# A two-layer linear-attention block on one core: the second layer's first weights are placed and split during the attention product, and operand places move

## The chip, the cores and the metric

The kernel runs on one core of a Trainium2 chip. A core has five engines with queues of their own: PE (matmul), DVE (vector), ACT (scalar), POOL and SP; all transfers run on 16 shared DMA engines, and here SP's queue issues the loads and POOL's queue most stores. The metric is the device time of one execution in microseconds, the median of several runs. Before the change it is 2347.4 us (three runs, 2346.8 to 2353.08).

## The reference

`x` is [1, 2048, 1024], all in fp32. D = 1024, F = 3584, 32 heads of 32.

```python
x = A_x
xn = _layernorm(x, axis=-1)
s = _A_ref(xn, A_wqkv, A_wo)                 # linear attention, then @ wo
g = _silu(_B_ref(xn, B_w1, B_w3, B_w2))      # (silu(xn@w1) * (xn@w3)) @ w2
return x + s * g
...
pq, pk = phi(q), phi(k)
kv = jnp.einsum("bhsd,bhse->bhde", pk, v)
z = jnp.einsum("bhsd->bhd", pk)
num = jnp.einsum("bhqd,bhde->bhqe", pq, kv)
den = jnp.einsum("bhqd,bhd->bhq", pq, z)[..., None] + 1e-6
o = num / den
return (lambda x, *d: x.transpose(*d))(o, 0, 2, 1, 3).reshape(B, S, D) @ wo
```

## The kernel before

*Arithmetic.* Every large product is cut in 2 by 2 blocks and done with seven block products in place of eight (their names are in PRODUCTS: B11, T2, T3, T1, B21, T4, B22 for the right operands, and their partners A11, S2, S3, S1, A12, A22, S4 for the left ones). Each fp32 operand is split in two fp32r parts: `split` (L91) makes the high part with a cast on ACT (L95) and the low part with a subtract on DVE (L96). `mm3` (L100) then does three matmuls: left high by right high (L103), left high by right low (L104), left low by right high (L105). So the first two of a product need only the cast of the left operand, and the third needs its subtract.

*Stages.* First q, k, v and gate and up products over two halves of the tokens, with intermediate results in DRAM. Then two right-hand products, both done by the class `Segment` (L1001): the attention product `attention` ("s", nk = 4: queries divided by their denominators times the weights merged with wo), and the second layer, cut in five segments `layers` ("B0" with nk = 2, "B1" to "B4" with nk = 3), which add up in the sums `acc`. B0 follows directly on the attention product.

*A segment.* `right(k)` (L1010) loads, places and splits the seven right operands of step k. `operands(m)` (L1017) loads and splits the seven left operands of token group m (256 tokens; there are NG = 8 groups): these are called XA11, XS2 and so on, with raw loads rA11, rS2. `tokens(m, ...)` (L1033) does the group's products in PSUM banks a, b, c, d and adds them up with ACT and DVE in u and the four sums. Group 0 of a segment is done "outer": over k first and over the seven products within, so that only the operands of one k must be there at a time. `run` (L1220) goes over the groups, one group ahead with `operands(m + 1)`; at the last group it calls `ahead()`, and in every group `around(m)` if given. So while PE does group m, the other engines prepare group m + 1.

*Names in the profile.* Buffer numbers are left out: `XA11s` is a left operand of the attention product, `XA11B` one of a second-layer segment; `as`, `bs`, `cs`, `ds` are its PSUM banks, `us` and `s` its sums, and `aB` to `dB`, `uB`, `acc` those of the second layer. `B<-rB11B` and `T<-rT2B` are splits of second-layer weights; `wp` are the attention product's right operands, split in the same way.

*Places.* Tiles come from pools. `pb` (8 places of 4 KB per partition) holds left operands, `pe` (3) u, `pc` ("c" 6 places: `small`; "sg" 4 places: `signed`) sums and raw loads. `pa` holds the operands of the first stages and then `wp`; `praw` raw loads; `st` little things. `pa`, `praw` and `st` are opened in `era1` and closed after the attention product (L1266). Only then is `pw` opened, at their addresses, for the second layer's right operands (`layer_place`, L1269) and `acc`. So `layers[0].right(0)` (L1278) stands behind the whole attention product; `ask_first` (L1160) has four of its seven raw loads issued during the last attention group, two into spare `pe` places and two into `small` ones. The constant tile "gap" (L63) does no work; it moves all later addresses.

*What sets the order.* A scheduler orders the instructions of each engine when the program is built, and engines are then in order: an instruction that waits holds up all behind it on its engine, and a load that waits for its place to be free holds up all later loads of SP's queue.

Of the kernel before, what the change touches and what calls it, by code (L numbers as in the profile page):

```python
# [9 lines left out]
F32 = mybir.dt.float32  # L10
FR = mybir.dt.float32r
# [5 lines left out]
P = 128  # L17
C = 512
# [4 lines left out]
def tile_linear_attention_times_swiglu(  # L23
# [23 lines left out]
    const = ctx.enter_context(tc.tile_pool(name="const", bufs=1))  # L47
# [12 lines left out]
    for i in range(P // DH):  # L60
        nc.vector.memset(hmask[i * DH:(i + 1) * DH, i * DH:(i + 1) * DH], 1.0)

    const.tile([P, 79], F32, name="gap")  # L63
    zacc = const.tile([P, ND], F32, name="zacc")
    nc.vector.memset(zacc, 0.0)

# [2 lines left out]
    PRODUCTS = ["B11", "T2", "T3", "T1", "B21", "T4", "B22"]  # L69
# [21 lines left out]
    def split(pair, src, bias=None):  # L91

        hi, lo = pair[:, 0], pair[:, 1]
        if bias is None:
            nc.scalar.copy(out=hi, in_=src)  # L95
            return nc.vector.tensor_sub(out=lo, in0=src, in1=hi.bitcast(F32))  # L96
        nc.scalar.activation(hi, src, AF.Identity, bias=bias)
        return nc.vector.scalar_tensor_tensor(lo, src, bias, hi.bitcast(F32), op0=ALU.add, op1=ALU.subtract)
# [9 lines left out]
    pb = ctx.enter_context(tc.tile_pool(name="pb", bufs=8))  # L108
    pe = ctx.enter_context(tc.tile_pool(name="pe", bufs=3))
    pc = ctx.enter_context(tc.tile_pool(name="pc", bufs=6))  # L110
    era1 = ExitStack()
    pa = era1.enter_context(tc.tile_pool(name="pa", bufs=1))
    praw = era1.enter_context(tc.tile_pool(name="praw", bufs=2))
    st = era1.enter_context(tc.tile_pool(name="st", bufs=2))

    def small(name):
        return pc.tile([P, C], F32, tag="c", name=name)
# [189 lines left out]
    def columns(w, c0, n):  # L307
        return w[:, c0:c0 + n].rearrange("(k p) n -> p k n", p=P)
# [3 lines left out]
    class Operands:  # L312
# [10 lines left out]
        def ask(self):  # L323
            if self.raw is None:
                self.raw = praw.tile([P, ND, 2 * P], F32, tag="raw", name=f"w{self.name}")
                fetched[:] = [nc.sync.dma_start(out=self.raw, in_=columns(self.w, self.c0, 2 * P))]
# [86 lines left out]
    jobs = []  # L413
# [561 lines left out]
    for h in range(NH):  # L975
        order = [(part, pair) for part in (1, 0) for pair in range(ND // 2)]
        if h:
            order = [(part, pair) for pair in range(ND // 2) for part in (1, 0)]
        some = [Operands(wqkv, part * D + pair * 2 * P, f"{'qk'[part]}{h}_{pair}_", h == 0 and part == 1,
                         h and part == 0 and pair == 0)  # L980
                for part, pair in order]
# [17 lines left out]
    NG = S // GT  # L999
    PARTNER = {"B11": "A11", "T2": "S2", "B21": "A12", "T3": "S3", "T1": "S1", "T4": "A22", "B22": "S4"}  # L1000
    class Segment:  # L1001


        def __init__(self, name, nk, first, last, place, right, left, acc, end=None):
            self.last, self.U = last, {}
            self.name, self.nk, self.first = name, nk, first
            self.place, self.right_of, self.left_of, self.acc, self.end = place, right, left, acc, end
            self.Y, self.X = {}, {}

        def right(self, k):  # L1010

            for i, n in enumerate(PRODUCTS):
                raw = self.right_of(n, i, k)
                self.Y[n, k] = self.place(n, i, k)
                split(self.Y[n, k], raw)
# [130 lines left out]
    def hiddens(i, m):  # L1146
        return left(m, lambda n: h_d[i][m // NT][:, PLACE[n][m % NT]], (FB[i][1] - FB[i][0]) // 2, f"B{i}")
# [7 lines left out]
    def second_weights(i, n, k):  # L1155
        if (i, n, k) not in asked:
            ask(i, n, k, small)
        return asked[i, n, k]

    def ask_first():  # L1160

        for n, place in zip(PRODUCTS, (spare, spare, small, small)):
            ask(0, n, 0, place)

    def spare(name):
        return pe.tile([P, C], F32, tag="u", name=name)
# [53 lines left out]
    def run(seg, nxt=None, ahead=None, around=None):  # L1220

        def between(k):
            if m == NG - 1 and nxt:
                if k == 0:
                    nxt.operands(0)
                    for e in range(seg.nk, nxt.nk):
                        nxt.right(e)
                if k < nxt.nk:
                    nxt.right(k)

        if not seg.X:
            seg.operands(0)
        for m in range(NG):
            if m + 1 < NG:
                seg.operands(m + 1)
            elif ahead:
                ahead()
            if around:
                around(m)
            seg.tokens(m, m == 0 or m == NG - 1 and nxt is not None, between)  # L1240
# [13 lines left out]
    def attention_place(n, i, k):  # L1254
# [3 lines left out]
    attention = Segment("s", ND // 2, True, True, attention_place,  # L1258
                        attention_right, queries, lambda m, t, n: small(f"s{m}_{t}{n}"), store_s)
    attention.operands(0)  # L1260
    for k in range(attention.nk):
        attention.right(k)
    run(attention, ahead=ask_first)
    assert all(next(j, None) is None for j, _ in jobs)
    jobs.clear()
    era1.close()  # L1266
    pw = ctx.enter_context(tc.tile_pool(name="pw", bufs=1, reuse_waits="tile"))

    def layer_place(n, i, k):  # L1269
        return pw.tile([P, 2, C], FR, tag=f"{n}_{k}", name=f"{n}_{k}")  # L1270

    acc = []
    layers = [Segment(f"B{i}", (f1 - f0) // 2, i == 0, i == len(FB) - 1, layer_place,
                      lambda n, _, k, i=i: second_weights(i, n, k),
                      lambda m, i=i: hiddens(i, m), lambda m, t, n: acc[m][:, t, n],
                      finish if i == len(FB) - 1 else None)
              for i, (f0, f1) in enumerate(FB)]
    layers[0].right(0)  # L1278
    layers[0].operands(0)
    for k in range(1, layers[0].nk):  # L1280
        layers[0].right(k)
    acc.extend(pw.tile([P, 2, 2, C], F32, tag=f"acc{m}", name=f"acc{m}") for m in range(NG))
    for i, seg in enumerate(layers):
        run(seg, layers[i + 1] if i + 1 < len(layers) else None, around=lay_x if i == 2 else None)

# [22 lines left out]
```

## Time and profile before

| what | value |
|---|---|
| median of three runs | 2347.4 us |
| the profiled execution | 2349.84 us |
| its span (first to last instruction) | 2348.1 us |
| mean granted TensorE clock | 0.996 |
| DMA traffic | 479.69 MB, mean 204 GB/s |

The profile is of one execution, which was somewhat slower than the median; a sum of parts is made against its span and then carried over to the median. Times in timeline rows are microseconds from the start of the span: start, duration, engine, line, operation, output<-inputs, shapes, and in brackets how long the engine had stood idle before and what ended that. Ends of matmuls are modelled (0.39 us each), so the pitch from start to start says how fast PE goes. SPq rows are loads being issued, not their landing. Some matmul records are missing from the trace, a few per cent, so counts of matmuls are taken from the program.

### The profile page before, as it was taken

The page shows a single profiled execution, that of the slowest core. Times are in us where ns is not written, and L with a number is a line of the kernel's source. Part 1 is how long each engine was busy: PE and PEld are TensorE (multiplying, and loading weights), DVE is VectorE, ACT ScalarE, POOL GpSimd, SP SyncE. Part 2 cuts the span into 40 slices and gives each one's busy share as a digit, 9 for nine tenths or more (in the row PEclk, how much of TensorE's full clock was granted, in tenths as well). Part 3 has the DMA queues.
Part 4 walks back from the last instruction along what each step waited for, and adds up shares of the span by engine and source line. Part 5 has one row for each costly group of instructions (what it writes and reads, how often), then busy time and mean ns, then how long its engine had stood idle before and what let it go on. Part 6 is the DMA issues. An engine that isn't in the chain of part 4 may idle for free.

```text
span 2348.1 us, 30976 instructions
## 1 busy us (share of the span) xinstructions
PE 2300.6 (98%) x10368; PEld 1890.5 (81%) x10368; DVE 1780.3 (76%) x2830; ACT 924.7 (39%) x1639; POOL 689.8 (29%) x854
## 2 busy tenths in 40 slices
PE   6999999999999999999999999999999999999997
PEld 5788888888887888777888888888887888888876
DVE  8887888888777775657867788887745666766798
ACT  5555343433232555433332433334324534242433
POOL 4220333376866221001423344342310000000033
PEclk9999999999999999999999999999999999999999
DMA  6555455576668646776756666665656566665688
GB/s 233 179 184 180 153 184 184 170 226 218 226 209 314 221 146 202 253 258 203 224 180 183 191 193 212 205 213 174 224 158 196 180 188 176 222 215 177 192 267 258
DMA packets 353695, 479.69 MB, mean 204 GB/s; under 512 B 24208, under 2 KB 262800, under 8 KB 353424
## 3 DMA queue, kind: packets, MB, share of 16 engines
q1 hardware_dynamic: 315808, 357.63, 48.2%
q0 software_dynamic: 37728, 120.09, 15.6%
q8 instruction: 81, 1.33, 0.2%
q14 instruction: 78, 0.64, 0.1%
HBM read 306.71 MB, written 174.59 MB: 205 GB/s over the span
## 4 chain that ended last, share of the span: by engine, by line
PE 73%; issue 5%; DVE 4%; DMA 3%; ACT 1%; POOL 0%; SPq 0%; DVEq 0%; POOLq 0%; ACTq 0%
PE g L103 2%; PE g L104 2%; PE g L105 2%; PE dB L104 1%; PE dB L105 1%; PE dB L103 1%; PE aB L103 1%; PE cB L103 1%; PE cB L104 1%; PE aB L104 1%; PE aB L105 1%; PE cB L105 1%; PE bB L105 1%; PE bB L104 1%; PE bB L103 1%
## 5 line engine op out<-in xcount | busy, mean ns | idle before, releaser
L750 POOL DMA_DIRECT2D h_d<-sg x112 | 82.8, 740 | 256.8 <-DVE sg L746 166.3
L1063 POOL DMA_DIRECT2D u_d<-uB x32 | 17.3, 541 | 407.6 <-DVE uB L1046 345.8
L96 DVE TENSOR_TENSOR xy<-xy,xy 128x512 fp32r<-128x512 f32 x112 | 72.9, 686 | 65.4 <-ACT xy L95 65.3
L95 ACT CAST xy<-xy 128x512 fp32r<-128x512 f32 x112 | 65.1, 619 | 102.0 <-PE g L105 58.4
L104 PE MATMUL g<-xy,xy 128*128 128x512 f32 x224 | 87.8, 392 | 0.3 <-DVE xy L96 0.2
L105 PE MATMUL g<-xy,xy 128*128 128x512 f32 x224 | 87.3, 390 | 0.0
L103 PE MATMUL g<-xy,xy 128*128 128x512 f32 x224 | 82.7, 398 | 0.0
L517 POOL DMA_DIRECT2D y_d<-y x48 | 34.6, 721 | 140.0 <-ACT y L537 79.9
L1046 DVE TENSOR_TENSOR acc<-cB,acc 128x512 f32<-128x512 f32 x50 | 34.4, 689 | 42.9 <-PE cB L105 42.9
L1046 DVE TENSOR_TENSOR acc<-dB,acc 128x512 f32<-128x512 f32 x56 | 38.6, 689 | 30.8 <-PE dB L105 30.6
L730 POOL TENSOR_TENSOR hs<-hs,sg 128x256 f32<-128x256 f32 x56 | 60.5, 1081 | 0.1
L732 POOL TENSOR_TENSOR hs<-sg 128x256 f32<-128x256 f32 x56 | 57.3, 1023 | 0.0
L103 PEld LDWEIGHTS g<-xy,xy 128*128 128x128 f32 x224 | 41.8, 188 | 14.2 <-issue 4.5
L888 POOL DMA_DIRECT2D qs_d<-qd x32 | 18.1, 564 | 117.5 <-DVE qd L884 80.1
L1177 POOL DMA_DIRECT2D s_d<-s x32 | 17.3, 541 | 117.4 <-DVE s L1046 69.2
L733 POOL TENSOR_TENSOR hs<-sg,hs 128x256 f32<-128x256 f32 x56 | 50.6, 903 | 1.4
L104 PEld LDWEIGHTS g<-xy,xy 128*128 128x128 f32 x224 | 42.1, 188 | 10.2 <-DVE xy L96 1.4
L729 POOL TENSOR_TENSOR hs<-sg,sg 128x256 f32<-128x256 f32 x56 | 49.7, 887 | 1.2
L765 POOL TENSOR_TENSOR w<-w 128x256 f32<-128x256 f32 x28 | 28.2, 1007 | 73.0 <-DMA w<-in_B_w 73.0
L105 PEld LDWEIGHTS g<-xy,xy 128*128 128x128 f32 x224 | 42.1, 188 | 8.8
L758 POOL DMA_DIRECT2D h_d<-hs x60 | 45.8, 765 | 3.5 <-POOL hs L733 2.4
L95 ACT CAST XS4B<-rS4B 128x384 fp32r<-128x384 f32 (+1 forms) x40 | 19.7, 493 | 60.7 <-PE cB L105 41.1
(5315 smaller groups left out, 8326.9 us busy)
## 6 DMA issues: line engine op xcount, KB each, us to landing
h_d<-hs POOLq DMA_DIRECT2D x60, 256.0 KB, 3.3
h_d<-sg POOLq DMA_DIRECT2D x56, 256.0 KB, 3.7
w<-in_B_w SPq DMA_DIRECT2D x56, 256.0 KB
wt_d<-w SPq DMA_DIRECT2D x28, 512.0 KB
xy<-x_d SPq DMA_DIRECT2D x28, 512.0 KB
xy<-y_d SPq DMA_DIRECT2D x28, 512.0 KB
h_d<-hs SPq DMA_DIRECT2D x52, 256.0 KB
y_d<-y POOLq DMA_DIRECT2D x48, 256.0 KB, 3.1
```

The costliest lines, as they stand in the source:

```text
L95: nc.scalar.copy(out=hi, in_=src)
L96: return nc.vector.tensor_sub(out=lo, in0=src, in1=hi.bitcast(F32))
L103: nc.tensor.matmul(acc, lhsT=wh, rhs=ah, start=start, stop=False, skip_group_check=True)
L104: nc.tensor.matmul(acc, lhsT=wh, rhs=al, start=False, stop=False, skip_group_check=True)
L105: return nc.tensor.matmul(acc, lhsT=wl, rhs=ah, start=False, stop=stop, skip_group_check=True)
L729: e.tensor_add(out=s1, in0=a21, in1=a22)
L730: e.tensor_sub(out=s2, in0=s1, in1=a11)
L732: e.tensor_sub(out=s3, in0=a11, in1=a21)
L733: e.tensor_sub(out=s4, in0=a12, in1=s2)
L750: nc.gpsimd.dma_start(out=h_d[i][2 * h + c][:, 2 * n:4 * n + 2, k], in_=src)
L758: queue.dma_start(out=h_d[i][2 * h + c][:, 6 + 4 * e:10 + 4 * e, k], in_=o[e].rearrange("p (e s) -> p e s", s=P))
L1046: return V.tensor_add(out=c, in0=src, in1=c)
```

## The change

`pa` moves from era1 into an era of its own and to the right end of SBUF; `praw` and `st`, now alone on the left, are closed before the attention product runs, once its last raw weights are split. Their room becomes `pw0`, which holds the seven k = 0 right operands of the second layer and acc0. During attention groups 2 to 6 a new hook, `first_weights`, calls `layers[0].right(0)` for one or two of the seven products (products 0 and 1 in group 2, 2 in group 3, 3 and 4 in group 4, 5 in group 5, 6 in group 6). At the last group `ask_next` issues four early loads as `ask_first` did, but for k = 1. The rest of the right operands and sums stay in `pw`, which takes the place of `pa`, on the right, after the attention product. An "edge" tile of 8 floats and a "gap" of 47 instead of 79 floats set the addresses: operand places, all at 64 modulo 512 before, are all at 448 modulo 512 after.

```diff
-    const.tile([P, 79], F32, name="gap")
+    const.tile([P, 47], F32, name="gap")
...
-    era1 = ExitStack()
-    pa = era1.enter_context(tc.tile_pool(name="pa", bufs=1))
+    era1, era2 = ExitStack(), ExitStack()
+    ctx.enter_context(tc.tile_pool(name="edge", bufs=1, side="right")).tile([P, 8], F32, name="edge")
+    pa = era2.enter_context(tc.tile_pool(name="pa", bufs=1, side="right"))
...
-        def right(self, k):
-
-            for i, n in enumerate(PRODUCTS):
+        def right(self, k, some=range(7)):
+
+            for i in some:
+                n = PRODUCTS[i]
                 raw = self.right_of(n, i, k)
...
-    def ask_first():
+    def ask_next():
 
         for n, place in zip(PRODUCTS, (spare, spare, small, small)):
-            ask(0, n, 0, place)
+            ask(0, n, 1, place)
...
-    run(attention, ahead=ask_first)
-    assert all(next(j, None) is None for j, _ in jobs)
+    era1.close()
     jobs.clear()
-    era1.close()
-    pw = ctx.enter_context(tc.tile_pool(name="pw", bufs=1, reuse_waits="tile"))
+    pw0 = ctx.enter_context(tc.tile_pool(name="pw0", bufs=1, reuse_waits="tile"))
+    pw = []
 
     def layer_place(n, i, k):
-        return pw.tile([P, 2, C], FR, tag=f"{n}_{k}", name=f"{n}_{k}")
+        return (pw[0] if k else pw0).tile([P, 2, C], FR, tag=f"{n}_{k}", name=f"{n}_{k}")
...
-    layers[0].right(0)
+
+    def first_weights(m):
+        if 2 <= m < NG - 1:
+            layers[0].right(0, [i for i in range(7) if i * 5 // 7 == m - 2])
+
+    run(attention, ahead=ask_next, around=first_weights)
     layers[0].operands(0)
+    era2.close()
+    pw.append(ctx.enter_context(tc.tile_pool(name="pw", bufs=1, side="right", reuse_waits="tile")))
     for k in range(1, layers[0].nk):
         layers[0].right(k)
-    acc.extend(pw.tile([P, 2, 2, C], F32, tag=f"acc{m}", name=f"acc{m}") for m in range(NG))
+    acc.append(pw0.tile([P, 2, 2, C], F32, tag="acc0", name="acc0"))
+    acc.extend(pw[0].tile([P, 2, 2, C], F32, tag=f"acc{m}", name=f"acc{m}") for m in range(1, NG))
```

## The prediction

> **What bounds the kernel now.** The page first: TensorE is busy for almost the whole span, so only time in which it stands still can be won.
>
> ```profile
> span 2348.1 us, 30976 instructions
> PE 2300.6 (98%) x10368; PEld 1890.5 (81%) x10368; DVE 1780.3 (76%) x2830; ACT 924.7 (39%) x1639; POOL 689.8 (29%) x854
> ```
>
> Then the busy time by stage (columns: stretch, length, then busy us and count of PE, PEld, DVE, ACT, POOL; granted clock, DMA share, GB/s). The stretches are the attention product, the change to the second layer, the rest of its first segment, its middle segments, its last one.
>
> ```profile
> 1640.90:1793.26 152.36, 151.79 (x669) 125.13 (x667) 82.41 (x122) 45.86 (x80) 28.86 (x45) 1.00 0.57 178
> 1793.26:1830.00 36.74, 32.70 (x137) 24.72 (x136) 27.82 (x52) 21.88 (x48) 2.16 (x4) 1.00 0.81 263
> 1830.00:1869.40 39.40, 39.40 (x176) 32.66 (x175) 21.94 (x46) 22.18 (x51) 2.16 (x4) 1.00 0.54 160
> 1869.40:2250.00 380.60, 380.60 (x1681) 315.57 (x1680) 273.22 (x471) 141.44 (x270) 21.77 (x32) 1.00 0.63 195
> 2250.00:2341.00 91.00, 83.94 (x365) 67.82 (x363) 83.16 (x140) 34.42 (x65) 28.99 (x33) 1.00 0.97 295
> ```
>
> PE is full in the attention product and from 1830 to 2250, and has holes from 1793 to 1830 and in the last segment, where the DMA engines are 97% busy. The change works in the first of these. The timeline of PE there, begun with two matmuls of the steady stream before it:
>
> ```profile
> 1779.66 0.39 PE L103 MATMUL cs<-wp,XS3s 128*128 128x512 f32 x1
> 1793.03 0.39 PE L105 MATMUL ds<-wp,XS4s 128*128 128x512 f32 x1
> 1793.26 0.39 PE L103 MATMUL B11B<-B,XA11B 128*128 128x512 f32 x1
> 1794.80 0.50 PE L104 MATMUL B11B<-B,XA11B 128*128 128x512 f32 x1 [0.93 <-DVE B L96]
> 1798.87 0.50 PE L103 MATMUL B22B<-B,XS4B 128*128 128x512 f32 x1 [1.03 <-ACT B L95]
> 1802.28 0.50 PE L103 MATMUL T2B<-T,XS2B 128*128 128x512 f32 x1 [0.38 <-ACT T L95]
> 1819.68 0.50 PE L103 MATMUL cB<-T,XS3B 128*128 128x512 f32 x1 [1.64 <-ACT XS3B L95]
> 1826.42 0.50 PE L103 MATMUL aB<-B,XA11B 128*128 128x512 f32 x1
> ```
>
> The first two rows are 59 starts apart: 13.37 / 59 = 0.2266 us each. In PE's order of the built program 120 matmuls lie between the starts at 1793.26 and 1826.42; they should take 27.19 us and take 33.16, so 5.97 us are lost. The waits at 1794.80, 1798.87 and 1802.28 are for weights of the second layer (B, T); each costs its idle time, 0.16 (the modelled end, 0.39, hides that much beyond the pitch) and 0.11 (the start behind it takes 0.50 in place of 0.39): 0.93 + 1.03 + 0.38 + 3 x 0.27 = 3.15 in all. The rest, some 2.8, hangs on the left operands of the next token groups (XS3B, XA11B).
>
> **The change, part by part.** *Moved:* seven weight loads of 256 KB, seven casts and seven subtracts (the k = 0 weights of segment B0). They now stand in attention groups 2 to 6, one or two a group. The k = 1 weights take their old places, and the four early loads fetch k = 1. The built program has the same instructions on every engine; the orders differ from attention group 2 to the fourth group of B0, and not elsewhere.
>
> Cost in the attention product:
>
> ```profile
> 1757.12 0.43 SPq L1153 DMA_DIRECT2D rB11B<-in_B_w  x1
> 1758.10 0.62 ACT L95 CAST XS2s<-rS2q 128x512 fp32r<-128x512 f32 x1 [2.10 <-PE as L105]
> 1758.75 0.69 DVE L96 TENSOR_TENSOR XS2s<-rS2q,XS2s 128x512 fp32r<-128x512 f32 x1 [2.03 <-ACT XS2s L95]
> 1758.62 0.58 ACT L1094 COPY us<-as 128x512 f32<-128x512 f32 x1
> 1775.40 0.54 POOL L1177 DMA_DIRECT2D s_d<-s  x1 [2.18 <-DVE s L1053]
> ```
>
> A split is 0.62 us of ACT and 0.69 of DVE, in gaps of some 2 us which recur with every product (2.72 us). On ACT the copy of `as` stands behind a weight's cast, which can wait for its load. Nothing needs that bank before B21 is added to it, three products or 8.2 us later; the slowest load below takes 5.5 us and is issued about 0.5 us before the group begins. On SP's queue only loads for the next group, 19 us away, stand behind. The `small` places that the weights take wait for stores of the group before, whose last is issued at 1775.40, 1.2 us into a group (group 7 begins at 1774.22, 84 matmuls before 1793.26), and lands some 3 us later, while a weight load comes at the group's end. So I price this at 0; what hides it is PE's own stream. Without that cover seven subtracts would cost 4.8 us.
>
> At the transition, the weights and what their loads depend on:
>
> ```profile
> 1794.07 0.68 DVE L96 TENSOR_TENSOR B<-rB11B,B 128x512 fp32r<-128x512 f32 x1
> 1794.66 0.69 DVE L96 TENSOR_TENSOR T<-rT2B,T 128x512 fp32r<-128x512 f32 x1
> 1798.20 0.62 ACT L95 CAST B<-rB22B 128x512 fp32r<-128x512 f32 x1 [1.02 <-DMA rB22B<-in_B_w]
> 1798.85 0.69 DVE L96 TENSOR_TENSOR B<-rB22B,B 128x512 fp32r<-128x512 f32 x1 [0.76 <-ACT B L95]
> 1797.93 0.32 SPq L1153 DMA_DIRECT2D rT3B<-wt_d  x1
> 1802.63 0.62 ACT L95 CAST T<-rT3B 128x512 fp32r<-128x512 f32 x1 [0.41 <-DMA rT3B<-wt_d]
> 1803.29 0.69 DVE L96 TENSOR_TENSOR T<-rT3B,T 128x512 fp32r<-128x512 f32 x1 [0.34 <-ACT T L95]
> ```
>
> The first four rows become k = 1 at the same times, since their loads wait for the same stores. PE has 21 matmuls of k = 0 ready and reaches k = 1 at 1793.26 + 21 x 0.2266 = 1798.02, its B22 at 1801.87, when the cast (to 1798.82) and the subtract (to 1799.54) are done. All 3.15 us of weight waits go. The last three rows become weights of segment B1, which PE does not need yet.
>
> *What is late next:* left operands of group 2. Their loads stand on SP behind waits for the splits of group 1.
>
> ```profile
> 1808.30 0.42 DVE L96 TENSOR_TENSOR XA12B<-rA12B,XA12B 128x256 fp32r<-128x256 f32 x1
> 1808.74 0.32 SPq L1135 DMA_DIRECT2D rS2B<-h_d  x1
> 1813.21 0.43 ACT L95 CAST XS2B<-rS2B 128x256 fp32r<-128x256 f32 x1
> 1813.96 0.39 SPq L1135 DMA_DIRECT2D rS3B<-h_d  x1
> 1819.22 0.40 ACT L95 CAST XS3B<-rS3B 128x256 fp32r<-128x256 f32 x1 [2.05 <-DMA rS3B<-h_d]
> 1820.11 0.32 SPq L1135 DMA_DIRECT2D rS4B<-h_d  x1
> 1825.61 0.41 ACT L95 CAST XS4B<-rS4B 128x256 fp32r<-128x256 f32 x1 [1.80 <-DMA rS4B<-h_d]
> ```
>
> These loads take 4.5, 5.3 and 5.5 us from issue to cast. In the new DVE order XS1B, three sums of acc0 and B1's T1 stand between the subtract of 1803.29 and XA12B. With 0.6 us from one long start to the next (1794.07 to 1794.66) and 0.4 for a short one, XA12B ends near 1807.2 instead of 1808.7. So rS2B goes out 1.5 us earlier and its cast is done near 1812.1. PE wants it as matmul 76: 1793.26 + 76 x 0.2266 = 1810.48. A new wait of 1.6 to 1.9, taken 1.75. XS3B: XA22B's subtract, five long operations later, ends near 1810.6 and lets rS3B go, so its cast ends near 1816.3; PE, delayed by 1.75, wants it (matmul 96) at 1816.8: 0. XA11B of group 3 (matmul 114, wanted near 1820.8): its load waits for XS1B's subtract, near 1817.5 (XS1B is loaded right behind XS3B), then takes 3 to 4.5 us: 0 to 1.5, taken 0.9. Slower starts behind waits (0.11 each) and small steps, 0.5. Sum lost 3.15 against 5.97: **2.8 us gained**. Bounds: 6.0 (no new wait, if loads take 3.5 us) and 0 (they take over 5.3 us throughout).
>
> *Addresses.* In the built program all operand places start at 64 modulo 512 before and at 448 after, so they lie to each other as they did. What a shift does to an engine is shown by one tile which already lies at 0 modulo 512, uk__342, beside one at 64:
>
> ```profile
> L447 ACT COPY uk__342<-ak__343 x1: 585/585/585, 23.1 to 23.1; 128x512 f32<-128x512 f32 x1
> L447 ACT COPY uk__365<-ak__366 x1: 587/587/587, 25.6 to 25.6; 128x512 f32<-128x512 f32 x1
> h_d<-sg POOLq DMA_DIRECT2D x56, 256.0 KB, 3.7
> s_d<-s POOLq DMA_DIRECT2D x12, 256.0 KB, 3.0
> q0 software_dynamic: 3296, 7.87, 29.6%
> ```
>
> 585 against 587 ns: nothing. No full-size matmul streams an operand from another address, and no transfer uses one; I take 0 for both, as for ACT. From above for transfers: a store of 256 KB in pieces of 512 bytes (h_d) lands after 3.7 us, one in whole rows of 2048 bytes (s_d) after 3.0, so being cut in four costs a row 23%, and a shift should not cost it more. From below a gain of as much is as open, but I have no reason for it.
>
> [...]
>
> **The rivals.** (A) *All of it comes back*: the loads get faster because seven fewer of them crowd the stretch from 1793 to 1830 (DMA share 0.81): 2347.4 - 6.0 = 2341.4. Against it: B1's loads move up into the room. (B) *The wait only moves*: the loads of groups 2 and 3 take 5.3 us or more, as rS3B and rS4B do, and what PE wins ahead it loses there: 2347.0. (C) *Slower, by the addresses*: transfers with a row at 448 take longer and the last segment, DMA 97% busy for 91 us (88 us of DMA work), is stretched. At 3.2% the gain is gone, from 11% the kernel is slower by 0.3%. At the bound of 23%: stores alone (29.6% of 108 us) 0.23 x 32 = 7.4, so 2352.0; all transfers 20.2, so 2364.8. For it: that stage leaves no room. Against it: the ACT row. A matmul slowed by the shift belongs here too: 0.1% of 2300 us is 2.3 us.
>
> **How the numbers follow.** The profiled execution took 2349.84 us for its span of 2348.1; less 2.8 that is 2347.0. Against the median of the runs, 2347.4, it is **2344.6**. Forecast 0.60 (its own range 2343.0 to 2346.4), A 0.11, B 0.15, C 0.14. 0.3% is 7.0 us, about what a measurement of this kernel can tell from no change (its runs lie 6.3 apart). Faster than that lies beyond even A: 0.04, for scatter. Slower than 2354.4: the upper part of C and scatter, 0.11. The same: 0.85. The range goes from just under A to the stores of C: 2341.0 to 2352.0.
>
> **What would show it.** Right: PE starts at a pitch of 0.2266 from 1793.26 to about 1810, first wait on XS2B of 1 to 2 us, no wait on B or T; full PE in the attention product with seven more splits in its gaps. Wrong: a wait of `cs` or `as` there (moved step not hidden), a matmul pitch other than 0.2266 or a longer landing of s_d<-s than 3.0 us (addresses), or a last segment that lasts longer than 91 us by more than its scatter.

## The result and the profile after

| kernel | median us | lowest to highest | runs |
|---|---|---|---|
| before | 2348.74 | 2346.64 to 2354.18 | 11 |
| after | 2343.29 | 2339.08 to 2346.91 | 11 |

The ratio is 0.9976, 95% interval 0.9966 to 0.9985: 5.5 us or 0.24% less, between 3.5 and 8.0 us by the interval. The forecast was 2344.6, a gain of 2.8 on the 2347.4 known then; the sign is right, the gain is about twice as large, and 2.8 lies just below the interval.

The page of the changed kernel, and its busy time by stage in the stretches used before (its attention product ends 2.4 us later, since this execution came to it later):

```profile
span 2345.1 us, 30980 instructions
PE 2300.3 (98%) x10368; PEld 1888.9 (81%) x10368; DVE 1780.5 (76%) x2830; ACT 923.9 (39%) x1639; POOL 687.0 (29%) x854
```

```profile
1640.90:1793.26 152.36, 151.86 (x670) 125.43 (x669) 88.32 (x132) 47.96 (x85) 28.65 (x45) 1.00 0.62 194
1793.26:1830.00 36.74, 35.45 (x154) 27.93 (x152) 25.53 (x51) 21.73 (x49) 2.70 (x5) 1.00 0.72 231
1830.00:1869.40 39.40, 39.40 (x175) 32.66 (x174) 21.25 (x45) 21.85 (x50) 2.16 (x4) 1.00 0.52 157
1869.40:2250.00 380.60, 380.60 (x1680) 315.13 (x1680) 274.32 (x473) 140.13 (x267) 21.82 (x33) 1.00 0.63 196
2250.00:2341.00 91.00, 83.31 (x359) 66.50 (x357) 82.86 (x139) 34.20 (x65) 28.93 (x33) 0.99 0.96 294
```

The attention product in its own stretch of this execution, 2.36 us later:

```profile
1643.26:1795.62 152.36, 151.86 (x671) 125.41 (x669) 86.82 (x129) 49.43 (x87) 28.84 (x45) 1.00 0.62 191
```

PE stays full there (151.86 of 152.36 us, 151.79 before), although DVE and ACT do more (129 instructions for 122, 87 for 80: the seven moved subtracts and casts). In the second row PE gains 2.75 us (35.45 for 32.70; its busy time counts modelled ends, so it shows less than the 3.7 us found below), and the DMA share falls from 0.81 to 0.72. The last row still has its holes.

The timeline of PE at the transition (start, duration, engine, line, operation; in brackets the idle time and its end):

```profile
1795.62 0.39 PE L103 MATMUL B11B<-B,XA11B 128*128 128x512 f32 x1
1804.91 0.39 PE L104 MATMUL T4B<-T,XA22B 128*128 128x512 f32 x1
1810.45 0.39 PE L105 MATMUL dB<-T,XS1B 128*128 128x512 f32 x1
1811.47 0.50 PE L103 MATMUL aB<-B,XA12B 128*128 128x512 f32 x1 [0.63 <-ACT uB L1096]
1814.71 0.50 PE L103 MATMUL bB<-T,XS2B 128*128 128x512 f32 x1 [0.66 <-ACT XS2B L95]
1823.73 0.50 PE L103 MATMUL aB<-B,XA11B 128*128 128x512 f32 x1
```

The second row is 41 matmuls behind the first: 9.29 / 41 = 0.2266 us each. So PE goes at full pitch through all of k = 0 and k = 1, and none of the three waits for B and T is left. The last row, XA11B of group 3, is matmul 114: 28.11 us behind the first, where 114 x 0.2266 = 25.83 were needed. Lost are 2.28 us; before, 5.97. Two waits make 1.8 of it, and their origin is seen on ACT and SP:

```profile
1806.38 0.40 ACT L95 CAST XS1B<-rS1B 128x256 fp32r<-128x256 f32 x1
1808.47 0.63 ACT L95 CAST B<-rB21B 128x512 fp32r<-128x512 f32 x1
1809.00 0.63 ACT L95 CAST T<-rT4B 128x512 fp32r<-128x512 f32 x1
1809.52 0.63 ACT L95 CAST B<-rB22B 128x512 fp32r<-128x512 f32 x1
1810.82 0.59 ACT L1096 COPY uB<-aB 128x512 f32<-128x512 f32 x1
1814.26 0.40 ACT L95 CAST XS2B<-rS2B 128x256 fp32r<-128x256 f32 x1 [1.74 <-DMA rS2B<-h_d]
...
1810.37 0.38 SPq L1137 DMA_DIRECT2D rS2B<-h_d  x1
```

From 1806.38 to the copy of bank a (uB) ACT has no idle time: weights of segment B1 (rB21B, rT4B, rB22B), which PE does not need before B1 begins at 1874.2, some 65 us later, stand ahead of a copy for which PE waits at 1811.47. And rS2B is issued at 1810.37 and cast 3.9 us later.

In the attention product the list of PE's waits (line waited for: us in all, times, longest) is as before, first the kernel after, then before:

```profile
PE cs L103 <- DVE s L1055: 0.5, 1, 0.5
```

```profile
PE cs L103 <- DVE s L1053: 0.5, 1, 0.5
```

A second difference lies in the last segment, at one wait for a sum; before, then after:

```profile
2293.82 0.50 PE L103 MATMUL cB<-T,XA22B 128*128 128x512 f32 x1 [3.09 <-DVE acc L1046]
```

```profile
2290.87 0.50 PE L103 MATMUL cB<-T,XA22B 128*128 128x512 f32 x1 [1.05 <-DVE acc L1048]
```

Three questions follow. Is the order of the splits the cause, or do the new places help by themselves? Is that wait in the last segment part of the gain? And do the addresses matter?

### The profile page after: what moved, and what is told of

The parts are those of the page before. It is cut to its first block, busy times and chain, and to the rows that moved or that the text cites. A ratio compares the mean times of both kernels' runs of the same rounds, so it can differ in the third digit from the quotient of the medians.

```text
span 2345.1 us, 30980 instructions
## 1 busy us (share of the span) xinstructions
PE 2300.3 (98%) x10368; PEld 1888.9 (81%) x10368; DVE 1780.5 (76%) x2830; ACT 923.9 (39%) x1639; POOL 687.0 (29%) x854
## 3 DMA queue, kind: packets, MB, share of 16 engines
q0 software_dynamic: 37728, 120.09, 15.8%
## 4 chain that ended last, share of the span: by engine, by line
PE 70%; DVE 5%; DMA 3%; issue 1%; ACT 1%; SPq 0%; DVEq 0%; ACTq 0%
PE g L103 2%; PE g L104 2%; PE g L105 2%; PE aB L105 1%; PE dB L103 1%; PE aB L103 1%; PE aB L104 1%; PE cB L105 1%; PE dB L104 1%; PE dB L105 1%; PE cB L104 1%; PE cB L103 1%; DMA rS4B<-h_d 1%; PE bB L103 1%; PE bB L104 1%
```

## The experiments

Each is timed against the kernel before on the same chip; ratios are to that kernel, taken over all runs and so not exactly those of the medians, with their 95% interval.

### The layout without the order

The places of the changed kernel; the k = 0 weights are loaded at the last group as before, and split behind B0's first left operands. The two marks (`ends`: the last cast and the last subtract of these operands) hold ACT's casts and DVE's subtracts of the weights back.

```diff
-            ask(0, n, 1, place)
+            ask(0, n, 0, place)
...
-    run(attention, ahead=ask_next, around=first_weights)
+    run(attention, ahead=ask_next)
     layers[0].operands(0)
+    with ExitStack() as behind:
+        for done in layers[0].ends:
+            behind.enter_context(tc.issue_after(done.ins))
+        layers[0].right(0)
```

> The layout of the changed kernel (operand places on the right, the gap and the edge, pw0 below pw, acc0 below) with the order of work of the kernel before: the weights of step 0 of B0 are asked for during the attention product and split only behind the operands of B0's group 0. Theory O (the gain is the order alone: the split weights are there when the attention ends): the time is that of before, 2348.7 +- 1 us, and the stretch from B0's first matmul to the 40 us behind it loses 5 to 6 us beyond the pitch, as before (5.75). Theory L (the layout brings part of it, in the last segment or along the way): 2346 to 2347 us, with a wait on the accumulator in the last segment near 1 us instead of 3.1. Theory A (the addresses cost something): above 2350 us.

Measured: 2348.1 against 2346.16, ratio 1.0003 (0.9995 to 1.0012). The waits for weights are back (PE's waits in the first 40 us of B0):

```profile
PE T4B L103 <- ACT T L95: 1.1, 1, 1.1
PE T2B L103 <- ACT T L95: 0.6, 1, 0.6
PE dB L103 <- ACT XS4B L95: 0.6, 1, 0.6
```

The right side, pw0 and the new addresses bring nothing alone that the runs show; the gain belongs to the order. The loss in these 40 us is only 3.7 us, under the 5 to 6 expected. Why it is less is not shown; one profile is one sample of when loads land.

### The addresses alone

The kernel before, with only its gap changed; the order of all instructions stays.

```diff
-    const.tile([P, 79], F32, name="gap")
+    const.tile([P, 47], F32, name="gap")
```

> The kernel before with the gap of 47 floats instead of 79, nothing else: every place on the left moves from 64 to 448 modulo 512, order and waits stay. Theory O: 2348.7 +- 1 us, no change. Theory L (places at 448 serve a transfer or an engine better than at 64): 2346 to 2347 us. Theory A, the rival of the prediction in which stores and loads become slower: 2350 us or more, with the last segment some 2 us longer.

Measured: 2348.39 against 2346.16, ratio 1.0006 (0.9996 to 1.0016). Transfers of the store queue (packets, MB, share of the 16 engines over the span; then landing of the s_d stores in us), first before, then this kernel:

```profile
q0 software_dynamic: 37728, 120.09, 15.6%
...
s_d<-s POOLq DMA_DIRECT2D x32, 256.0 KB, 3.0
```

```profile
q0 software_dynamic: 37728, 120.09, 15.8%
...
s_d<-s POOLq DMA_DIRECT2D x32, 256.0 KB, 2.9
```

Moving all places together from 64 to 448 costs the store queue about 1% (15.8 for 15.6) and its landing nothing. Rival C, as the prediction priced it (3.2% and more), does not occur. The time alone would not decide, as the 2.8 us at which C takes the whole gain lie inside the interval (0.9 us less to 3.8 us more).

### One side out of step

The changed kernel with 8 floats more in the gap: the left side moves to 480, the right side stays at 448. No instruction changes its place in any queue.

```diff
-    const.tile([P, 47], F32, name="gap")
+    const.tile([P, 55], F32, name="gap")
```

> The changed kernel with the gap of 55 floats instead of 47: the places on the left stand at 480 modulo 512, those on the right stay at 448, so that there is no common address; order and waits stay those of the changed kernel. Theory O: 2343.3 +- 1 us. Theory L with the common address as what matters: 1 to 3 us slower, 2344.5 to 2346, anywhere along the span.

Measured: 2389.31 against 2346.16, ratio 1.0181 (1.0164 to 1.0197): some 46 us slower than the changed kernel, fifteen times the most that either theory allowed for. The timeline of PE in group 0 of B0 shows where:

```profile
1828.95 0.40 PE L103 MATMUL B11B<-B,XA11B 128*128 128x512 f32 x1
1829.18 0.39 PE L104 MATMUL B11B<-B,XA11B 128*128 128x512 f32 x1
...
1833.49 0.39 PE L105 MATMUL B22B<-B,XS4B 128*128 128x512 f32 x1
1833.71 0.40 PE L103 MATMUL B11B<-B,XA11B 128*128 128x512 f32 x1
...
1838.38 0.40 PE L104 MATMUL T4B<-T,XA22B 128*128 128x512 f32 x1
```

The first 21 matmuls are those of k = 0, whose weights lie in pw0 on the left, like the left operands: from 1828.95 to 1833.49 there are 20 starts, 0.227 us each. From 1833.71 on comes k = 1, with the moving operand in pw on the right and the stationary one on the left: 20 starts in 4.67 us, 0.233 each. No wait lies between. Products of the same kind, for the same tokens, run 2.8% slower. The stages ahead, which also pair the two sides (the first products and the attention product), run at 0.232 to 0.2335 in the median, so that B0 begins 33 us later than in the changed kernel; from there to the last matmul it takes 9 us more. So what counts is how the two operands lie to each other. The next runs look at this alone.

### All places in step at 480, and other steps

> The changed kernel with all operand places, left and right, at 480 modulo 512 (gap of 55 floats, no edge tile), so one common place that is no multiple of 64. Theory C: pitch 0.2266 throughout and the time of the changed kernel +- 1. Theory U: pitch near 0.233 everywhere, 2385 us or more.

```diff
-    const.tile([P, 47], F32, name="gap")
+    const.tile([P, 55], F32, name="gap")
...
-    ctx.enter_context(tc.tile_pool(name="edge", bufs=1, side="right")).tile([P, 8], F32, name="edge")
+    pass
```

Then the changed kernel with other gaps and the edge as it is: 79 floats (the change without its edit of the gap), 63 and 111.

> The changed kernel without its edit of the gap (79 floats as before): places on the left at 64 modulo 512, places on the right at 448, a step of 128 bytes between the two; order and waits are those of the changed kernel. Theory C (TensorE's pitch suffers wherever its stationary and its moving operand stand at different places modulo 512): as with the left side at 480, a pitch near 0.233 us wherever the two come from different sides, and 2385 to 2392 us. Theory U (it suffers only where an operand doesn't stand on a multiple of 64 bytes): pitch 0.2266 throughout, and the time of the changed kernel +- 1.

> The changed kernel with a gap of 63 floats: places on the left at 0 modulo 512, on the right at 448, a step of 64 bytes. If any step modulo 512 between the two operands of a matmul slows it: pitch 0.231 to 0.233 us and 2382 to 2390 us, as with steps of 32 and of 128 bytes. If only the step modulo 64 or modulo 128 counted, 128 would have been as fast as none, so this run would add nothing; if the slowing shrinks with the step, 64 lies between the 45 us of step 32 and the 39 us of step 128.

> The changed kernel with a gap of 111 floats: places on the left at 192 modulo 512, on the right at 448, a step of 256 bytes. Theory 512 (only places that agree modulo 512 give the short pitch): 0.231 to 0.233 us and 2382 to 2390 us. Theory 256 (places have to agree modulo 256 only): pitch 0.2266 and the time of the changed kernel, 2344 +- 2.

| left, right (modulo 512) | step | pitch of B0's k = 1, us | median us | ratio to before |
|---|---|---|---|---|
| 448, 448 (after) | 0 | 0.2267 | 2343.29 | 0.9976 (0.9966 to 0.9985) |
| 480, 480 | 0 | 0.2267 | 2344.16 | 0.9979 (0.9970 to 0.9987) |
| 480, 448 | 32 | 0.2331 | 2389.31 | 1.0181 (1.0164 to 1.0197) |
| 0, 448 | 64 | 0.2322 | 2389.22 | 1.0173 (1.0143 to 1.0202) |
| 64, 448 | 128 | 0.2318 | 2384.36 | 1.0153 (1.0139 to 1.0167) |
| 192, 448 | 256 | 0.2267 | 2341.97 | 0.9969 (0.9958 to 0.9981) |

The pitch is the time of 20 starts from the first of k = 1 on, unrounded, divided by 20; three of these matmuls are of group 1 with k = 0, whose operands both lie on the left. Its rows for the step of 128 bytes (first and last, 20 starts apart), and behind them for 256:

```profile
1833.72 0.40 PE L103 MATMUL B11B<-B,XA11B 128*128 128x512 f32 x1
...
1838.35 0.39 PE L104 MATMUL T4B<-T,XA22B 128*128 128x512 f32 x1
```

```profile
1800.23 0.39 PE L103 MATMUL B11B<-B,XA11B 128*128 128x512 f32 x1
...
1804.76 0.39 PE L104 MATMUL T4B<-T,XA22B 128*128 128x512 f32 x1
```

4.63 us against 4.53. Theory C holds and U falls: 480 is no multiple of 64 and costs nothing if both sides stand there (0.2267); a step between two multiples of 64 costs it all (0.2322 and 0.2318). And of the last pair, theory 256 holds: with places that agree modulo 256 and not modulo 512 (192 and 448, the one such pair that was run) the pitch is 0.2267. Whether the loss grows smaller from 32 to 128 the ratios do not say, since their intervals overlap. The attention product says it, where every matmul pairs the two sides. The start of its last group, 84 matmuls ahead of B0's first, with a step of 128 bytes and then in the changed kernel:

```profile
1809.33 0.39 PE L103 MATMUL as<-wp,XA11s 128*128 128x512 f32 x1
...
1828.93 0.39 PE L103 MATMUL B11B<-B,XA11B 128*128 128x512 f32 x1
```

```profile
1776.58 0.39 PE L103 MATMUL as<-wp,XA11s 128*128 128x512 f32 x1
...
1795.62 0.39 PE L103 MATMUL B11B<-B,XA11B 128*128 128x512 f32 x1
```

These 84 take 19.60 us against 19.04, and 19.60 as well at steps of 32 (1809.35 to 1828.95) and 64 (1806.31 to 1825.91): 0.2333 us each for 0.2267, the same loss of 2.9% at all three steps.

The gap of 63 shows one thing more. Its left places are at 0 modulo 512, and the store queue is busy for less of the span (packets, MB, share of the 16 engines):

```profile
q0 software_dynamic: 37728, 120.09, 13.4%
```

That is 320 us of its span of 2387.6, where it was 366 us before (15.6% of 2348.1) and is 370 to 373 with the left places at 192, 448 or 480. So where the left places start does count for this queue: 13% less at 0 than at 64, but hardly a difference between 64 and 448. It is one profile, and not every landing is shorter (y_d 2.6 us for 3.1, s_d 3.2 for 3.0). What all places at 0, in step, would bring was not run.

### B1's weights behind the next groups

What the changed kernel still loses at the start of B0 was put down to B1's weights ahead of the operands of groups 1 and 2. Here their loads stand behind the last operand load of group 2.

```diff
+            if (name, m) == ("B0", 2):
+                held[:] = loads
...
-        nc.sync.dma_start(out=t, in_=second_weight(i, n, k))
+        with ExitStack() as behind:
+            if i == 1:
+                behind.enter_context(tc.issue_after(held[0].ins))
+            nc.sync.dma_start(out=t, in_=second_weight(i, n, k))
```

> The changed kernel, with the weight loads of segment B1 held on SP behind the last operand load of B0's group 2; their casts and subtractions follow the loads. Theory O, with what is left at the start of B0 (2.3 us in the profile, at the copy of the first bank to u and at XS2B of group 1) put down to B1's weights standing ahead of group 1 on SP, ScalarE and VectorE: these waits fall to under 0.5 us, no new wait when B1 starts, and 2341.3 +- 1 us. Rival: the copy and XS2B wait for something else (the bank's last matmul, the transfer itself): the 2.3 us stay and the time is 2343.3. Second rival: B1's weights then come late for B1's first group: slower than 2343.3, with waits on B or T near 1870 us.

Measured: 2340.02 against 2346.16, ratio 0.9976 (0.9967 to 0.9984). That is no better than the changed kernel's ratio in its own comparison, on other runs, so both were then run on one chip:

> The changed kernel once more, unaltered, beside the kernels below on one chip. Theory O (what the change gives is the 3.7 us of the first matmuls of B0, all else is scatter): 3.7 us under before +- 1, a ratio of 0.9984, loss in the 40 us from B0's first matmul again 2 to 2.5 us, and the last segment's wait on the accumulator anywhere between 0.5 and 3.5 us. Theory P (the last segment gains too, by something that the change does there): 5 to 6 us under before, with that wait again near 1 us.

> The kernel with B1's weight loads behind group 2 of B0 once more, to set it against the changed kernel on the same chip. If its 2.3 us are worth their full size: 2 to 2.5 us under the changed kernel of this call. If they come back later (the last segment, scatter): no difference that the runs show.

| on one chip | median us | ratio to before |
|---|---|---|
| before | 2348.29 | |
| the changed kernel again | 2344.93 | 0.9981 (0.9972 to 0.9990) |
| B1's weights behind group 2 | 2342.76 | 0.9968 (0.9958 to 0.9979) |

The medians lie 2.2 us apart, as expected; the two intervals overlap in their ends, so the size is known to a microsecond or two. The changed kernel itself is 3.4 us under before by the medians and 4.5 by the ratio, so this second comparison does not part the two theories of its expectation; its loss at the start of B0 is 1.55 us, under the 2 to 2.5 expected. The profile shows the late weights more sharply (the first 36.74 us of B0; the changed kernel, then the one with late weights):

```profile
1795.62:1832.36 36.74, 35.45 (x153) 27.97 (x152) 26.30 (x52) 21.43 (x50) 2.70 (x5) 1.00 0.74 235
```

```profile
1794.36:1831.10 36.74, 36.74 (x164) 30.42 (x163) 26.67 (x53) 21.63 (x50) 2.70 (x5) 1.00 0.73 241
```

PE is busy throughout and waits for nothing, neither here nor when B1 begins. The same load, copy and cast as above now come earlier:

```profile
1804.25 0.32 SPq L1137 DMA_DIRECT2D rS2B<-h_d  x1
1805.49 0.59 ACT L1096 COPY uB<-aB 128x512 f32<-128x512 f32 x1
1806.41 0.41 ACT L95 CAST XS2B<-rS2B 128x256 fp32r<-128x256 f32 x1 [0.33 <-DMA rS2B<-h_d]
```

From B0's first start, rS2B goes out after 9.9 us instead of 14.8 and is cast 2.2 us later instead of 3.9, and the copy starts after 11.1 us instead of 15.2. So both remaining waits came from B1's weights. The loads, casts and subtracts of these weights moved together, so which of them held rS2B back the runs do not part. By its ratio this kernel is level with the changed kernel at a gap of 111 (0.9969), compared on another chip; only the profile parts them at the start of B0, where 0 and 1.85 us are lost.

### What the last segment has to do with it

Each profile is also a sample of the second layer. The three kernels out of step are left out. From its PE timeline: B0's first start, the start of the last matmul, the difference, and the time lost beyond the pitch of 0.2266 in the first 40 us of B0.

| kernel | first | last | difference | lost in 40 us |
|---|---|---|---|---|
| before | 1793.26 | 2338.15 | 544.89 | 5.75 |
| before, gap of 47 | 1793.52 | 2338.71 | 545.19 | 6.95 |
| layout without the order | 1792.71 | 2335.94 | 543.23 | 3.68 |
| after | 1795.62 | 2335.20 | 539.58 | 2.27 |
| after, again | 1794.11 | 2333.81 | 539.70 | 1.55 |
| after, all at 480 | 1793.77 | 2333.90 | 540.13 | 2.12 |
| after, gap of 111 | 1795.47 | 2334.51 | 539.04 | 1.85 |
| B1's weights late | 1789.76 | 2327.11 | 537.35 | 0 |
| B1's weights late, again | 1794.36 | 2331.45 | 537.09 | 0 |

Means: 544.4 with the order of before, 539.6 with that of after, 4.8 less; of these 5.46 - 1.95 = 3.5 us are in the first 40 us. Some 1.3 us come from further on, and all of that is in the last segment, PE being full in between. The wait for a sum there, in the layout without the order, in before with a gap of 47, in after again and in after with a gap of 111:

```profile
PE cB L103 <- DVE acc L1048: 2.6, 1, 2.6
```

```profile
PE cB L103 <- DVE acc L1046: 1.3, 1, 1.3
```

```profile
PE cB L103 <- DVE acc L1048: 0.6, 1, 0.6
```

```profile
PE cB L103 <- DVE acc L1048: 1.2, 1, 1.2
```

With 3.1 and 1.0 in the first two profiles, the order of before gives 3.1, 2.6 and 1.3, that of after 1.0, 0.6, 1.2 and none, and with B1's weights late it is 1.2 and 1.7. The sets barely part, and no instruction of the last segment changes its place in a queue.

The two smallest, 0.6 and none, have a cause of their own. In these two profiles (after again, and all at 480) the granted clock falls for 3.4 us in the last segment: over 2255 to 2260 it is 0.72 and 0.78 in the mean, over the next 5 us 0.93 and 0.87, where the other seven have 1.00. Matmuls then start every 0.43 us, so PE comes to the sum later and has less to wait for. By these clocks each of the two lost some 1.75 us (an estimate). How much of that the shorter waits gave back is not shown; if nothing, the part of the gain from further on is 2.2 us instead of 1.3. That one to two us of the gain lie in the last segment is likely, but not settled.

## Why the prediction was right, and where it was off

- *The weight waits go (3.15 us).* Right: PE keeps its pitch of 0.2266 through k = 0 and k = 1, and without the order two waits for T return.
- *Nothing is paid in the attention product.* Right: PE's busy time and its one wait of 0.5 us are the same with the splits in the gaps. The cover is PE's own stream.
- *What is late next (1.75 at XS2B).* The time is right, the place only half. Without the slow starts behind them, which the prediction counted among its small steps, the two waits cost 1.61 us: 0.79 at the copy of bank a (0.63 idle and 0.16 hidden by the modelled end) and 0.82 at XS2B (0.66 and 0.16). The prediction followed the loads on SP and the subtracts on DVE past the moved weights of B1, but not the copies on ACT. Its date for XS2B held by luck. B0 begins 2.36 us later than in the profile before; so shifted, rS2B should have been issued at 1809.60 and its cast have ended at 1814.46. It was issued at 1810.37, 0.8 us later, and cast 3.9 us after, not 4.5, so the cast ended at 1814.66. PE could not go on before that, so by these rows the missed wait at the copy only took the place of part of the wait at XS2B.
- *XA11B of group 3 (0.9).* The term that was mis-sized: PE starts it 0.29 us after the matmul ahead of it, so 0.06 is lost there. Its load was issued at 1820.34 and its cast began at 1823.27, 2.9 us later, less than the 3 to 4.5 of the forecast. The slow starts and small steps make the other 0.61 (forecast 0.5), and the sum is 2.28 in place of 3.15.
- *The gain at the transition (2.8).* Measured 3.7 in the two profiles (5.97 - 2.28), 3.5 over the means of three and four. The rest of the 5.5 lies in the last segment, which the prediction left unchanged, and in what runs differ by: measured again, the whole gain was 4.5 us by the ratio, between 2.3 and 6.6.
- *The addresses (0).* Right, and by the right clause: "so they lie to each other as they did". That clause carried more than the prediction knew. Its rival C looked for the cost in transfers and in one common shift, where 64 to 448 moves about 1% of the store queue; the cost, 40 to 47 us, sits in matmuls whose operands stand out of step, and the edits of gap and edge avoid it. The price set on a slower matmul, 0.1%, was nearly 30 times too small for that case (2.9%). The sign that was named for the addresses, s_d landing later than 3.0 us, cannot tell: it is 3.1 and 3.2 in the two profiles after, and 2.9 where only the addresses changed.
- *Rivals.* A (all 6 us come back) did not happen in this kernel, whose transition still loses 2.3; it does with B1's weights behind group 2. B (the wait only moves) fell: 2.28 us are lost where 5.97 were. C (slower by the addresses) did not happen in this kernel either.

## What to carry to other kernels

When weights are prepared earlier, follow what takes their old place through every queue, the copies that free a bank included: here the next segment's weights, not needed for some 65 us, took back 2.3 us until they too were moved. Keep the stationary and the moving operand of a matmul at places that agree modulo 256 bytes before judging a new layout (of the steps tried, 0 and 256 gave 0.2267 us from start to start, 32, 64 and 128 gave 0.2318 to 0.2333); out of step the same order was 1.7 to 2.0% slower, and nothing in the list of waits tells of it, only the pitch from start to start. And profile each variant: the loss at the transition scatters from 3.7 to 7.0 us in the three profiles of one order and from 1.6 to 2.3 in the four of the other, so a single pair could have shown a gain anywhere between 1.4 and 5.4; the means give 3.5.

## What was not expected of the hardware

In these runs a 128x512 matmul started every 0.2266 to 0.2267 us where its two operands' places differ by 0 or 256 bytes modulo 512, and every 0.2333 us at steps of 32, 64 and 128 bytes (attention product), at a granted clock of 0.99 or more over the span in both. Within one execution (gap of 55 floats), products of two operands of the left side kept the short pitch (20 starts in 4.54 us) while those across the sides had the long one (20 starts in 4.67 us). So the pitch went with how the two operands' addresses lie to each other; by what mechanism, the runs do not show.
